# Token-major z1 and spatial product, with the gated product turned by DMA, in a fused state-space and gMLP kernel

## The chip, the cores and the metric

The kernel runs on one core of one Trainium2 chip. The metric is device microseconds (us) of that core. Before the change the median was 384.5 us over four runs (381.9 to 388.1). The run whose trace was kept took 377.6 us (a span of 375.8), less than any of these four, so comparisons with the trace of the kernel before are off by up to some 2%. Runs of one kernel scatter by 1 to 2% here; a run more than 1.5% above the fastest of its kernel is called slow, and ratios use fast runs alone: the mean time of one kernel's fast runs over the mean of the other's in the same rounds, so a ratio is not quite the quotient of the medians quoted beside it.

Engines: PE is the tensor engine (PEld its weight loads), DVE the vector engine, ACT the scalar engine, POOL is GpSimd, SP the engine whose queue issues most transfers.

## The reference, cut to what matters

```python
x = A_u                                           # [1, 2048, 640], bf16
g = sigmoid((x * gate_w).sum(-1, keepdims=True))
a = ssm_conv(x, ...)                              # long convolution, done by FFT
z = gelu(x @ w_in)                                # [2048, 1728]
z1 = z[..., :864];  z2 = layernorm(z[..., 864:])
s = einsum('ts,bsf->btf', w_sp, z2) + b_sp[None, :, None]     # the spatial product, [2048, 864]
b = (z1 * s) @ w_out                              # [2048, 640]
return g * a + (1 - g) * b
```

`a` needs tables of complex exponentials (DVE, ACT and POOL make them in four parts), a transform of the tables, and a convolution. `b` is nearly all matmuls. The kernel weaves the two together: the matmuls of `b` fill PE while the tables are made.

## The kernel before

Every piece of work is a task with an assumed cost. A planner in the kernel file plays the tasks through once, when the kernel is built, and fixes the order of instructions on each engine. At run time each engine follows its list in order, waiting where data or a buffer is missing. The parts that the change touches:

```python
class Plan:
    SYNC = 0.12                      # assumed wait between engines
# ...
def z1_tile(ft, hf):                 # features on partitions: 7 tiles of 128 (the last of 96), 2 halves of tokens
    # ...
    pe.matmul(ps()[0:fs, h, :], lhsT=Win1[:, i, 128*ft:128*ft+fs], rhs=xT[:, i, 1024*hf+512*h:...+512], ...)
    # GELU into zt, stored to z1_d in 512-byte rows
# ...
def sp_block(tb):                    # 8 blocks of 256 tokens
    # wT: the transposed rows of w_sp; z1t: z1 from z1_d; br: the biases as a row
    for st in range(c0, c0 + 4):
        pe.matmul(ps()[0:fs, ft - f0, :], lhsT=z2n[:, st, 128*ft:128*ft+fs], rhs=wT()[:, st, :], ...)
    if c0 + 4 == NS:                 # the bias: a product one row deep
        pe.matmul(ps()[0:fs, ft - f0, :], lhsT=ones[0:1, 0:fs], rhs=br()[:], start=False, stop=True)
    # ...
    vec.tensor_tensor(out=v_()[:], in0=ps()[:], in1=z1t()[:, f0:f0 + 2, :], op=ALU.mult)
    # v_ has features on partitions: it is the stationary operand of the output product as it stands
    pe.matmul(ps()[:], lhsT=vT[ft // 2]()[0:fs, ft % 2, 128*r:128*r+128], rhs=Wout[0:fs, ft, ...], ...)
```

## Time and profile before

| | before |
|---|---|
| span of the profiled run | 375.8 us |
| PE, DVE, ACT, POOL busy | 327.5, 281.4, 249.9, 163.5 us |
| mean granted PE clock | 0.971 |
| spatial product | 896 matmuls of 256 columns and 56 bias matmuls |
| four batches of table transforms (`ps_k`) start at | 128.2, 164.8, 213.2, 255.9 us |
| 480-wide convolution products `p` on DVE, first to last start | 265.1 to 328.3 us |

### The profile page before, as it was taken

To read this page: it belongs to the slowest core of one execution; us is meant where nothing else is said; L and a number is where in the kernel's file an instruction comes from. 1 tells how busy PE (TensorE), PEld (TensorE's weight loads), DVE (VectorE), ACT (ScalarE), POOL (GpSimd) and SP (SyncE) were. 2 spreads that over 40 slices of the span, in tenths; PEclk is the share of its full clock that TensorE was granted. 3 is DMA by queue.
4 is the path that set the end of the run, shared out by engine and by line. 5 is a ranking of instruction groups with operands and counts; after the bars stand their busy time and mean duration, and the time that the engine had idled before them with its cause. 6 is when DMAs were issued, how large, how long until landed. Compare 5 with 4: busy or idle time off the path is not lost.

```text
span 375.8 us, 9357 instructions
## 1 busy us (share of the span) xinstructions
PE 327.5 (87%) x3688; PEld 229.6 (61%) x3688; DVE 281.4 (75%) x554; ACT 249.9 (67%) x474; POOL 163.5 (44%) x167
## 2 busy tenths in 40 slices
PE   0897799995999989997899979997998999999981
PEld 0353344442777867776777857676675775788750
DVE  3298999874699999996489956892546676877574
ACT  3443955667998889995797968631246666767573
POOL 5265889990639884624512155300659200000000
PEclk9999999999899999998999989999699999999997
DMA  8794157899967035383679843694474856211364
GB/s 211 152 173 174 44 166 225 262 280 246 197 181 182 4 70 128 80 187 69 148 128 319 162 103 79 105 258 151 75 180 128 240 165 228 65 37 54 106 179 104
DMA packets 96325, 56.83 MB, mean 151 GB/s; under 512 B 66580, under 2 KB 91856, under 8 KB 96280
## 3 DMA queue, kind: packets, MB, share of 16 engines
q1 hardware_dynamic: 92264, 47.84, 51.7%
q0 software_dynamic: 4016, 8.39, 8.6%
q8 instruction: 29, 0.48, 0.6%
q14 instruction: 16, 0.13, 0.1%
HBM read 24.73 MB, written 19.47 MB: 118 GB/s over the span
## 4 chain that ended last, share of the span: by engine, by line
PE 45%; DVE 21%; DMA 10%; ACT 7%; issue 6%; SPq 5%; POOL 5%; DVEq 0%; POOLq 0%; ACTq 0%
PE ps_g L643 10%; PE ps_z L578 7%; PE ps_o L665 6%; SPq L306 5%; PE ps_v L973 4%; PE ps_s2k L961 3%; PE ps_z L549 3%; PE ps_k L799 2%; DMA fu<-FU_d 2%; PE ps_k L800 2%; DVE ET L782 2%; DMA bs<-in_B_b_sp_dram 2%; DMA obr<-ob_d 2%; ACT ET L311 2%; PE ps_s1k L885 2%
## 5 line engine op out<-in xcount | busy, mean ns | idle before, releaser
L643 PE MATMUL ps_g<-wT,z2n 128*128 128x256 bf16 (+1 forms) x896 | 118.1, 279 | 7.9 <-DVE ma L721 5.1
L643 PEld LDWEIGHTS <-z2n 128*128 128x128 bf16 (+1 forms) x896 | 88.7, 104 | 27.5 <-issue 8.7
L963 DVE TENSOR_TENSOR p<-ps_s2k,us 128x960 bf16<-128x960 f32 (+1 forms) x48 | 48.5, 1042 | 22.7 <-PE ps_s2k L961 10.9
L318 ACT CAST us<-ps_u 128x480 bf16<-128x480 f32 (+1 forms) x44 | 22.6, 526 | 31.0 <-PE ps_u L950 20.6
L977 ACT CAST vt<-ps_v 120x512 bf16<-120x512 f32 (+1 forms) x48 | 27.6, 586 | 15.9 <-PE ps_v L973 15.7
L549 PE MATMUL ps_z<-Win,xT 128*128 128x432 bf16 (+1 forms) x160 | 32.9, 363 | 3.7 <-DVE gl L558 2.4
L665 PE MATMUL ps_o<-Wout,vT 128*128 128x320 bf16 (+1 forms) x224 | 35.1, 304 | 0.0
L578 PE MATMUL ps_z<-xT,Win 128*128 128x512 bf16 (+1 forms) x140 | 33.8, 379 | 0.0
L311 ACT ACTIVATE mr<-lre 128x160 bf16<-128x160 f32 x128 | 31.6, 323 | 0.0
L973 PE MATMUL ps_v<-G,p 128*120 128x128 bf16 (+1 forms) x384 | 29.2, 220 | 0.8 <-DVE p L963 0.3
L973 PEld LDWEIGHTS <-p 128*120 128x120 bf16 (+1 forms) x384 | 26.7, 127 | 4.6 <-DVE p L963 1.4
L549 PEld LDWEIGHTS <-xT 128*128 128x128 bf16 x160 | 16.1, 101 | 20.5 <-issue 8.5
L306 POOL DMA_DIRECT2D FK_d<-s1k x14 | 13.5, 967 | 34.4 <-ACT s1k L318 18.5
L665 PEld LDWEIGHTS <-vT 128*128 128x128 bf16 (+1 forms) x224 | 21.8, 99 | 8.7
L255 POOL TENSOR_SCALAR si<-th 128x160 int32<-128x160 f32 x25 | 16.8, 673 | 23.1 <-ACT mr L311 19.2
L311 ACT ACTIVATE ET<-ci 128x640 bf16<-128x640 int16 x36 | 25.0, 727 | 1.8 <-DVE ci L255 1.8
L311 ACT ACTIVATE z2n<-ps_z 128x864 bf16<-128x864 f32 x16 | 14.2, 891 | 17.5 <-PE ps_z L549 13.3
L799 PE MATMUL ps_k<-ET 128*32 128x33 bf16 x640 | 20.7, 238 | 5.2 <-issue 5.1
L257 POOL TENSOR_SCALAR z2n<-z2n,mv,rstd 128x864 bf16<-128x864 bf16 x7 | 24.8, 3553 | 0.3
L961 PE MATMUL ps_s2k<-fk,T 128*128 128x480 bf16 (+1 forms) x128 | 24.4, 307 | 0.3 <-ACT ot L1177 0.3
L578 PEld LDWEIGHTS <-Win 128*128 128x128 bf16 (+1 forms) x140 | 14.2, 101 | 15.7 <-issue 1.1
L800 PEld LDWEIGHTS <-ET 128*32 128x32 bf16 x640 | 19.7, 143 | 5.8 <-issue 5.8
(176 smaller groups left out, 677.3 us busy)
## 6 DMA issues: line engine op xcount, KB each, us to landing
FK_d<-s1k POOLq DMA_DIRECT2D x14, 320.0 KB, 5.2
FU_d<-s1u SPq DMA_DIRECT2D x16, 240.0 KB, 3.8
fu<-FU_d SPq DMA_DIRECT2D x16, 240.0 KB, 4.1
fk<-FK_d SPq DMA_DIRECT2D x16, 240.0 KB, 4.1
z_d<-zt SPq DMA_DIRECT2D x6, 512.0 KB, 4.9
z1t<-z_d SPq DMA_DIRECT2D x8, 384.0 KB
xf<-in_A_u_dram SPq DMA_DIRECT2D x8, 320.0 KB, 3.9
ob_d<-ob SPq DMA_DIRECT2D x12, 160.0 KB, 3.8
```

The lines of the kernel that those rows point to most:

```text
L306: E_[e].dma_start(out=out_(), in_=in_())
L311: return add("ACT", cost, lambda e: act.activation(out=out_(), in_=in_(), func=func, scale=scale), r=r, w=w, fset=fs, bias=bias, deps=deps)
L549: pe.matmul(ps()[:, h, 0:432 + h], lhsT=xT[:, i, 128 * st:128 * st + 128], rhs=Win2[:, i, 432 * h:432 * h + 432 + h], start=(i == 0), stop ...
L578: pe.matmul(ps()[0:fs, h, :], lhsT=Win1[:, i, 128 * ft:128 * ft + fs], rhs=xT[:, i, 1024 * hf + 512 * h:1024 * hf + 512 * h + 512], start= ...
L643: pe.matmul(ps()[0:fs, ft - f0, :], lhsT=z2n[:, st, 128 * ft:128 * ft + fs], rhs=wT()[:, st, :], start=(st == 0), stop=False)
L665: pe.matmul(ps()[:], lhsT=vT[ft // 2]()[0:fs, ft % 2, 128 * r:128 * r + 128], rhs=Wout[0:fs, ft, HD * h:HD * h + HD], start=(ft == 0), sto ...
L799: pe.matmul(o_, lhsT=X["ET"][:, 0:32, d], rhs=X["M2"][:, :, d], start=True, stop=False, tile_position=(0, 32 * q))
L800: pe.matmul(o_, lhsT=X["ET"][:, NA:NA + 32, d], rhs=X["E2"][:, :, d], start=False, stop=True, tile_position=(0, 32 * q))
L961: pe.matmul(ps()[:, i, W * n:W * n + W], lhsT=TK(k + n, i), rhs=fk()[:, j + n, :], start=True, stop=True)
L963: add("DVE", dv1(2 * NW), lambda e, p12=p12, ps=ps, ua=ua: vec.tensor_tensor(out=p12()[:, :, 0:NW], in0=ps()[:, :, 0:NW], in1=ua().unsquee ...
L973: pe.matmul(pv()[0:CH, 128 * (NK * c + n):128 * (NK * c + n) + 128], lhsT=p12()[:, i, W * n + CH * c:W * n + CH * c + CH], rhs=GV(k + n, i ...
L977: (vec.tensor_copy if e == "DVE" else act.copy)(out=X["vt"][h][0:CH, :, :, 4 * k:4 * k + 4 * NK], in_=pv()[0:CH, :].rearrange("p (c z m) - ...
```

## The change

The intent is to cut PE's work. z1 and the spatial product are made with tokens on partitions: 432 columns per matmul instead of 256, no partly filled seventh feature tile, and the bias, now one number per partition, is added in the DVE operation that multiplies by z1. The price is that the gated product v now has tokens on partitions and must be turned before the output product: a transposing DMA from SBUF to SBUF, one per 128 tokens. v has one buffer. The core of the diff:

```diff
-    def z1_tile(ft, hf):
+    def z1_tile(st):
-                    pe.matmul(ps()[0:fs, h, :], lhsT=Win1[...], rhs=xT[...512 columns], ...)
+                    pe.matmul(ps()[:, h, 0:432], lhsT=xT[:, i, 128 * st:128 * st + 128], rhs=Win1[:, i, 432 * h:432 * h + 432], ...)
+        zt = sbt(lambda: eev, "zt", "zt", [P, Fh], bufs=3)
...
+    def sp_tile(n):
+        wT = sbt(lambda: gsp, "wT", "wT", [P, NS, P], bufs=4)
+        dma("SP", lambda: z1t()[:], lambda: z1v[:, n, :], ..., r=[("z1", st) for st in range(NS)], ...)
+        v_ = sbt(lambda: gsp, "v", "v", [P, 896], bufs=1)
+        add("POOL", 0.2, lambda e: pool.memset(v_()[:, Fh:896], 0.0), w=[(v_, "p")], bias=9000)
+                        pe.matmul(ps()[:, 0:432], lhsT=wT()[:, st, :], rhs=z2n[:, st, 432 * h:432 * h + 432], ...)
+            vec.scalar_tensor_tensor(out=v_()[:, 432 * h:...], in0=ps()[:, 0:432], scalar=bsf[:, n:n + 1],
+                in1=z1t()[:, 432 * h:...], op0=ALU.add, op1=ALU.mult)
+        vT = sbt(lambda: gsp, "vT", "vT", [P, 7, P], bufs=2)
+            dma("SP", lambda: vT()[:], lambda: v_()[:], 229000, r=vr, w=[vT], tr=True, bias=5000)
...
-            pv = (gps if k % 99 == 0 else xps)("ps_v", [P, 512])
+            pv = (gps if k % 1 == 0 else xps)("ps_v", [P, 512])
```

(Cut: names, costs, unchanged arguments and the numbers of buffers. Also cut: the planner's priority of the DVE operation that makes v, and of the operation that takes the output product out of PSUM, falls from 9500 to about 400. The last pair moves the convolution's `ps_v` to the PSUM banks that the spatial product uses.)

More of the change, by code (lines that the diff above doesn't have):

```diff
@@ L279 @@
     KB_d = [dram.tile([129, w], BF, name=f"KB_d{g}") for g, w in enumerate(KW)]
-    z1_d = dram.tile([8, P, NFT, 256], BF, name="z1_d")
+    z1_d = dram.tile([L, Fh], BF, name="z1_d")
+    v_d = dram.tile([NS, P, 896], BF, name="v_d")
     ob_d = dram.tile([P, NS, D], BF, name="ob_d")
-    br_d = dram.tile([NS, P], BF, name="br_d")
     ctx.enter_context(tc.manual_schedule())
@@ L337 @@
     short = sbpool(short_s, "short", 1, "right")
-    for nm, n in (("dummy", 1), ("kk", 2), ("ti", 2), ("two", 2), ("g", 2), ("x", 2), ("wT", 2), ("z1t", 2), ("vT", 4), ("ob", 2), ("br", 2),
-                  ("xf", 2), ("s1u", 5), ("zt", 2), ("bst", 2), ("jk", 2), ("kg", 1)):
+    for nm, n in (("dummy", 1), ("kk", 2), ("ti", 2), ("two", 2), ("g", 2), ("x", 2), ("wT", 4), ("z1t", 3), ("vT", 2), ("v", 1), ("ob", 2),
+                  ("xf", 2), ("s1u", 5), ("zt", 3), ("bst", 2), ("jk", 2), ("kg", 1)):
         ring(nm, n)
@@ L410 @@
     c64 = bits("c64", 6, 1)
-    ones = const.tile([1, P], BF, name="ones")
-    vec.memset(ones[:], 1.0)
     mhalf = const.tile([P, NS], F32, name="mhalf")
@@ L448 @@
     vec.memset(gl[:, NS:32], 0.0)
-    bt16 = early.tile([NS, P], BF, name="bt16")
+    bsf = const.tile([P, NS], F32, name="bsf")
     psm = xps("pt_s", [P, 1024], BF)
     add("PE", 0.1, lambda e: pe.transpose(out=psm()[:, 0:ND], in_=gw5[:], identity=ident[0:ND, 0:ND]), r=["gw5", "pre3"], w=[psm], bias=6000)
-    add("PE", 0.1, lambda e: pe.transpose(out=psm()[0:NS, 128:256], in_=bs16[:], identity=ident[:]), r=["bs16"], w=[(psm, 1)], bias=6000)
     S_(add("DVE", 0.2, lambda e: vec.tensor_copy(out=Win2[:, :, Fh:Fh + 1], in_=psm()[:, 0:ND].unsqueeze(2)), r=[psm], w=["gwt"], bias=6000))
-    add("DVE", 0.2, lambda e: vec.tensor_copy(out=bt16[:], in_=psm()[0:NS, 128:256]), r=[(psm, 1)], w=["bt16"], bias=6000)
-    dma("POOL", lambda: br_d[:], lambda: bt16[:], 4096, r=["bt16"], w=["br_d"])
+    E(add("POOL", 0.3, lambda e: pool.tensor_copy(out=bsf[:], in_=bs16[:]), r=["bs16"], w=["bsf"], bias=3000))
     th = parm.tile([P, D], F32, name="th")
@@ L568 @@
     z1_ids, z2_ids, xb = [], {}, {}
-    XB = {13: 38}
-    def z1_tile(ft, hf):
-        fs = fsz[ft]
+    XB = {15: 38}
+    def z1_tile(st):
         ps = two("ps_z1")
@@ L577, in m @@
                 for i in range(ND):
-                    pe.matmul(ps()[0:fs, h, :], lhsT=Win1[:, i, 128 * ft:128 * ft + fs], rhs=xT[:, i, 1024 * hf + 512 * h:1024 * hf + 512 * h + 512],
+                    pe.matmul(ps()[:, h, 0:432], lhsT=xT[:, i, 128 * st:128 * st + 128], rhs=Win1[:, i, 432 * h:432 * h + 432],
                               start=(i == 0), stop=(i == ND - 1))
-            E(add("PE", 5 * mm(512), m, r=["Win1", ("xT", 2 * hf + h)], w=[(ps, h)], bias=3000 - 100 * (2 * ft + hf) - h))
-        if hf == 0:
-            zth[ft] = sbt(lambda: eev, "zt", "zt", [P, NS, P], bufs=2)
-        zt = zth[ft]
-        z1_ids.append(actf(ac(1024), lambda: zt()[0:fs, :, 64 * hf:64 * hf + 64].rearrange("f n (e p) -> f n e p", e=2),
-                           lambda: ps()[0:fs, :, :].rearrange("f e (p n) -> f n e p", n=NS), ACT.Gelu_apprx_tanh, [(ps, 0), (ps, 1), "dt16", "pre"], [(zt, hf)], bias=9000, deps=next((xb[t] for t in range(2 * ft + hf, -1, -1) if t in xb), [])))
-        if hf == 1:
-            E(dma("SP", lambda: z1_d[:, 0:fs, ft, :].rearrange("b p t -> p b t"), lambda: zt()[0:fs, :, :].rearrange("f (b r) t -> f b (r t)", r=2), 524000, r=[(zt, 0), (zt, 1)],
-                   w=[("z1", tb, ft) for tb in range(8)], bias=5000, run=512))
-    zth = {}
+            E(add("PE", 5 * mm(432), m, r=["Win1", ("xT", st // 4)], w=[(ps, h)], bias=3000 - 100 * st - h))
+        zt = sbt(lambda: eev, "zt", "zt", [P, Fh], bufs=3)
+        z1_ids.append(actf(ac(864), lambda: zt()[:].rearrange("p (e f) -> p e f", e=2), lambda: ps()[:, :, 0:432], ACT.Gelu_apprx_tanh,
+                           [(ps, 0), (ps, 1), "dt16", "pre"], [zt], bias=9000, deps=next((xb[t] for t in range(st, -1, -1) if t in xb), [])))
+        E(dma("SP", lambda: z1_d[128 * st:128 * st + 128, :], lambda: zt()[:], 221000, r=[zt], w=[("z1", st)], bias=5000, run=1728))
     xfh = {}
@@ L621 @@
     wspv = B_w_sp.rearrange("(p n) s -> p n s", n=NS)
-    brv = br_d[:].rearrange("n p -> (n p)").unsqueeze(0)
+    z1v = z1_d[:].rearrange("(p n) f -> p n f", n=NS)
     def sp_block(tb):
-        wT = sbt(lambda: gsp, "wT", "wT", [P, NS, 256])
-        for r in range(2):
-            dma("SP", lambda r=r: wT()[:, :, 128 * r:128 * r + 128], lambda r=r: wspv[:, 2 * tb + r, :], 540000, r=["xf3"], w=[(wT, r)], tr=True, bias=1000 - 100 * tb)
-        z1t = sbt(lambda: gsp, "z1t", "z1t", [P, NFT, 256])
-        dma("SP", lambda: z1t()[:, 0:6, :], lambda: z1_d[tb, :, 0:6, :], 393000, r=[("z1", tb, f) for f in range(6)], w=[(z1t, 0)], bias=1000 - 100 * tb, run=3072)
-        dma("SP", lambda: z1t()[0:96, 6, :], lambda: z1_d[tb, 0:96, 6, :], 49000, r=[("z1", tb, 6)], w=[(z1t, 1)], bias=1000 - 100 * tb, run=512)
-        br = sbt(lambda: gsp, "br", "br", [1, 256])
-        dma("SP", lambda: br()[:], lambda: brv[:, 256 * tb:256 * tb + 256], 512, r=["br_d"], w=[br], bias=1000 - 100 * tb)
-        vT = []
-        for f0 in range(0, NFT, 2):
-            ps = gps("ps_g", [P, 2, 256])
-            fts = range(f0, min(NFT, f0 + 2))
-            for ft in fts:
-                fs = fsz[ft]
-                for c0 in range(0, NS, 4):
-                    def m(e, ft=ft, fs=fs, ps=ps, f0=f0, c0=c0):
-                        for st in range(c0, c0 + 4):
-                            pe.matmul(ps()[0:fs, ft - f0, :], lhsT=z2n[:, st, 128 * ft:128 * ft + fs], rhs=wT()[:, st, :], start=(st == 0), stop=False)
-                        if c0 + 4 == NS:
-                            pe.matmul(ps()[0:fs, ft - f0, :], lhsT=ones[0:1, 0:fs], rhs=br()[:], start=False, stop=True)
-                    add("PE", (4 + (c0 + 4 == NS)) * mm(256), m, r=([(wT, 0), (wT, 1), br] if c0 == 0 else [wT, br]) + ([(ps, f0)] if ft > f0 and c0 == 0 else []) + [("z2n", s) for s in range(c0, c0 + 4)], w=[(ps, ft)], bias=-1000 - 100 * tb)
-            v_ = sbt(lambda: gsp, "vT", "vT", [P, 2, 256], bufs=4)
-            if f0 < 6:
-                add("DVE", dv1(512), lambda e, v_=v_, ps=ps, f0=f0: vec.tensor_tensor(out=v_()[:], in0=ps()[:], in1=z1t()[:, f0:f0 + 2, :], op=ALU.mult),
-                    r=[(ps, f) for f in fts] + [(z1t, 0)], w=[v_], bias=9500)
-            else:
-                add("DVE", dv1(256), lambda e, v_=v_, ps=ps: vec.tensor_tensor(out=v_()[0:96, 0, :], in0=ps()[0:96, 0, :], in1=z1t()[0:96, 6, :], op=ALU.mult),
-                    r=[(ps, f) for f in fts] + [(z1t, 1)], w=[v_], bias=9500)
-            vT.append(v_)
-        for r in range(2):
-            n = 2 * tb + r
-            late = tb >= 6
-            ob = (lambda n=n: X["obx"][:, n - 12, :]) if late else sbt(lambda: gsp, "ob", "ob", [P, D])
-            for h in range(2):
-                ps = xps("ps_o", [P, HD])
-                def m(e, r=r, h=h, ps=ps):
-                    for ft in range(NFT):
-                        fs = fsz[ft]
-                        pe.matmul(ps()[:], lhsT=vT[ft // 2]()[0:fs, ft % 2, 128 * r:128 * r + 128], rhs=Wout[0:fs, ft, HD * h:HD * h + HD],
-                                  start=(ft == 0), stop=(ft == NFT - 1))
-                add("PE", 7 * mm(HD), m, r=vT + ["Wout0", "Wout1"] + (["vap"] if late else []), w=[ps], hold_=[] if late else [ob], bias=-1000 + 5 - 100 * tb)
-                add("ACT", 0.53, lambda e, ob=ob, h=h, ps=ps, n=n: act.activation(out=ob()[:, HD * h:HD * h + HD], in_=ps()[:], func=ACT.Copy, scale=omg[:, n:n + 1]),
-                    r=[ps, "omg"], w=[("obx", n, h) if late else (ob, h)], bias=9500)
-            if not late:
-                dma("SP", lambda ob=ob, n=n: ob_d[:, n, :], lambda ob=ob: ob()[:], 164000, run=1280, r=[(ob, 0), (ob, 1)], w=[("ob", n)])
@@ new lines, in sp_block, with m @@
+        for n in (2 * tb, 2 * tb + 1):
+            sp_tile(n)
+    def sp_tile(n):
+        B0 = -50 * n
+        wT = sbt(lambda: gsp, "wT", "wT", [P, NS, P], bufs=4)
+        dma("SP", lambda: wT()[:], lambda: wspv[:, n, :], 540000, r=["xf3"], w=[wT], tr=True, bias=1000 + B0)
+        z1t = sbt(lambda: gsp, "z1t", "z1t", [P, Fh], bufs=3)
+        dma("SP", lambda: z1t()[:], lambda: z1v[:, n, :], 221000, r=[("z1", st) for st in range(NS)], w=[z1t], bias=1000 + B0, run=1728)
+        v_ = sbt(lambda: gsp, "v", "v", [P, 896], bufs=1)
+        add("POOL", 0.2, lambda e: pool.memset(v_()[:, Fh:896], 0.0), w=[(v_, "p")], bias=9000)
+        for h in range(2):
+            ps = gps("ps_g", [P, 512])
+            for c0 in range(0, NS, 4):
+                def m(e, ps=ps, c0=c0, h=h):
+                    for st in range(c0, c0 + 4):
+                        pe.matmul(ps()[:, 0:432], lhsT=wT()[:, st, :], rhs=z2n[:, st, 432 * h:432 * h + 432], start=(st == 0), stop=(st == NS - 1))
+                add("PE", 4 * mm(432), m, r=[wT] + [("z2n", s) for s in range(c0, c0 + 4)], w=[ps], bias=-1000 + B0)
+            add("DVE", dv1(432), lambda e, ps=ps, h=h: vec.scalar_tensor_tensor(out=v_()[:, 432 * h:432 * h + 432], in0=ps()[:, 0:432], scalar=bsf[:, n:n + 1],
+                in1=z1t()[:, 432 * h:432 * h + 432], op0=ALU.add, op1=ALU.mult), r=[ps, z1t, "bsf"], w=[(v_, h)], bias=400 + B0)
+        vT = sbt(lambda: gsp, "vT", "vT", [P, 7, P], bufs=2)
+        vr = [(v_, "p"), (v_, 0), (v_, 1)]
+        if False:
+            dma("SP", lambda: v_d[n], lambda: v_()[:], 229000, r=vr, w=[("vd", n)], bias=5000, run=1792)
+            dma("SP", lambda: vT()[:], lambda: v_d[n], 229000, r=[("vd", n)], w=[vT], tr=True, bias=5000)
+        else:
+            dma("SP", lambda: vT()[:], lambda: v_()[:], 229000, r=vr, w=[vT], tr=True, bias=5000)
+        late = n >= 12
+        ob = (lambda: X["obx"][:, n - 12, :]) if late else sbt(lambda: gsp, "ob", "ob", [P, D])
+        for h in range(2):
+            ps = xps("ps_o", [P, HD])
+            def m(e, h=h, ps=ps):
+                for ft in range(NFT):
+                    fs = fsz[ft]
+                    pe.matmul(ps()[:], lhsT=vT()[0:fs, ft, :], rhs=Wout[0:fs, ft, HD * h:HD * h + HD], start=(ft == 0), stop=(ft == NFT - 1))
+            add("PE", 7 * mm(HD), m, r=[vT, "Wout0", "Wout1"] + (["vap"] if late else []), w=[ps], hold_=[] if late else [ob], bias=-1000 + 50 + B0)
+            add("ACT", 0.53, lambda e, h=h, ps=ps: act.activation(out=ob()[:, HD * h:HD * h + HD], in_=ps()[:], func=ACT.Copy, scale=omg[:, n:n + 1]),
+                r=[ps, "omg"], w=[("obx", n, h) if late else (ob, h)], bias=400 + B0)
+        if not late:
+            dma("SP", lambda: ob_d[:, n, :], lambda: ob()[:], 164000, run=1280, r=[(ob, 0), (ob, 1)], w=[("ob", n)])
@@ L993 @@
     done_ = []
-    for i in range(2 * NFT):
-        z1_tile(i // 2, i % 2)
+    for i in range(NS):
+        z1_tile(i)
         if i < 8:
@@ L1053 @@
     kg2_s = ExitStack()
-    add("NONE", 0.0, open_cvt, w=["cvt"], deps=early_ids, r=["HT", "br_d", "gwt", "bt16"])
+    add("NONE", 0.0, open_cvt, w=["cvt"], deps=early_ids, r=["HT", "bsf", "gwt"])
     t_ids = []
```

## The prediction

> **What bounds the kernel now.** I read the page first (busy shares, slices, groups), then the stretches of 20 us, the tensor engine's waits and timeline, then the transposes. The page says that the tensor engine (PE) is the fullest, and that the spatial product is its largest user:
>
> ```profile
> PE 327.5 (87%) x3688; PEld 229.6 (61%) x3688; DVE 281.4 (75%) x554; ACT 249.9 (67%) x474; POOL 163.5 (44%) x167
> ...
> PE   0897799995999989997899979997998999999981
> ...
> DVE  3298999874699999996489956892546676877574
> ...
> L643 PE MATMUL ps_g<-wT,z2n 128*128 128x256 bf16 (+1 forms) x896 | 118.1, 279 | 7.9 <-DVE ma L721 5.1
> ```
>
> The reader is to see a PE row of nines from slice 10 on, and one group, L643 (the spatial product), with a third of PE's busy time. It is spread as filler from 94.7 us to 328.1 us, beside the tables (DVE nearly full from 120 to 160 us) and then beside the convolution. In the view by stretches:
>
> ```profile
> 140.00:160.00 20.00, 19.56 (x158) 14.99 (x156) 19.79 (x40) 18.81 (x30) 9.94 (x7) 1.00 0.46 109
> ...
> 280.00:300.00 20.00, 18.74 (x172) 13.37 (x171) 13.17 (x13) 12.49 (x24) 13.88 (x25) 1.00 0.68 188
> 300.00:320.00 20.00, 19.05 (x174) 13.32 (x173) 13.43 (x13) 12.50 (x24) 0.89 (x1) 1.00 0.63 201
> ```
>
> The columns are start:end and length, then busy us of PE, PEld, DVE, ACT, POOL, then clock, DMA share and GB/s. PE has 19 of 20 us in the convolution stage, where DVE and ACT have 13: there PE sets the pace, and each us of filler taken away shortens the stage. Before 90 us the chain of waits runs through z1 on PE; after about 345 us the end is evictions and output, which the change does not touch.
>
> The busy sum overstates PE, since ends of pipelined matmuls are modelled. So I take start-to-start distances from PE's timeline:
>
> ```profile
> 199.08 1.91 PE L643 MATMUL ps_g<-wT,z2n 128*128 128x256 bf16 x16
> 200.92 0.28 PE L645 MATMUL ps_g<-br,ones 1*128 1x256 bf16 x1
> 201.13 0.61 PE L643 MATMUL ps_g<-wT,z2n 128*128 128x256 bf16 x4
> 201.67 0.28 PE L645 MATMUL ps_g<-br,ones 1*128 1x256 bf16 x1
> 201.88 0.72 PE L885 MATMUL ps_s1k<-xk,F 128*128 128x320 bf16 x4
> ```
>
> Here the columns are start us, us to the last end, engine, line and group. Sixteen products take 1.84 us until the bias matmul (L645, one row deep) starts, and four take 0.54 us. The difference, 1.30 us for twelve, is 108 ns each; the fixed rest is about 0.1 us, and the bias matmul then holds PE for 0.21 us more. So one bias matmul costs about 0.3 us, three times a real product of the same width. That is the largest thing that the change removes.
>
> **What the Trainium skill says.** "TensorE: Matmul & The Clock Gate", section Back-to-back issue gap, gives N/2.4 + 2.5 ns for a warm isolated gap: 109.2 ns for 256 columns, 182.5 for 432, 215.8 for 512. The trace agrees: 108 ns above, and in the chain ten z1 matmuls of 512 columns take 2.16 us. That section has nothing on the bias matmul; 0.3 us is the trace's. "DMA: Bandwidth & Descriptors", section DMA Transpose (X-bar), asks for a destination in SBUF, 2-byte type and partitions in multiples of 16; the new transpose (128 rows of 896 bf16) fits. The same page, section Latency and other measured facts, gives 261 GB/s for a transposing DMA; this trace is slower, 524288 bytes per 2.79 us of the queue's time, 188 GB/s, so I use the trace:
>
> ```profile
> L304 SPq DMA_TRANSPOSE wT<-in_B_w_sp_dram x16: 2087/2791/4768, 82.5 to 244.1; - x16
> ...
> DMA to landing us min/median/max: 4.7/5.7/6.0
> ```
>
> **The change part by part.** All 16 token tiles now have their own spatial product of 2 x 16 matmuls of 432 columns, and the result has tokens on partitions.
>
> Spatial product on PE. Before: 896 x 109 ns = 97.7 us, plus 56 bias matmuls x 0.3 us = 16.8 us, together 114.5. After: 512 x 182.5 ns = 93.4 us; the bias goes into the DVE operation. Saved: 21.1 us. About 3.5 us of it is the padding of the seventh tile (96 of 128 rows used), about 17 the bias.
>
> z1 on PE. Before: 140 x 216 = 30.2 us. After: 160 x 182.5 = 29.2 us. Saved: 1.0 us, in the stage from 52 to 90 us where PE is on the chain. Weight loads are not a new limit: 97 ns each for xT, hidden below 182 ns. ACT: 14 x 1.024 = 14.3 us becomes 16 x about 0.89 (z2's duration for the same 864 elements) = 14.2 us.
>
> Output product: 224 matmuls of 320 columns, unchanged.
>
> DVE. Before: 24 x 0.691 + 8 x 0.410 = 19.9 us. After: 32 scalar_tensor_tensor of 432 from PSUM. The kernel's own one of 480 (L1151) takes 0.713 us, so about 0.66 us each, 21 us. Added: 1.2 us.
>
> DMA. z1 goes out and in with rows of 1728 bytes instead of 512 out: slightly better in the stretch from 82 to 95 us, where the DMA share is 1.01. New are 16 transposes of 128 x 896, 224 KB. The two transposes in the trace, 160 KB (1.27 us of queue, 3.5 us to landing) and 512 KB (2.79 and 5.7), give by a straight line about 1.55 us of queue and 3.9 us to landing. The SP queue has room: 16 x 1.55 = 25 us against over 190 us that it spends waiting. None is on a DMA limit, but each stands between a product and its output product, which used to need one DVE operation of 0.7 us.
>
> Smaller parts. The bias transpose and its trip through DRAM disappear from the start, where PE runs the gate's transpose at 11.0 us and the bias's at 11.3: about 0.3 us. The first product waits 5.1 us before 94.7 us; the second half of wT was issued at 89.15 us and lands 5.7 us later, at 94.8, so that is the true releaser. One token tile of wT now suffices. But all of z1 must have been stored before the first z1t can load, so the two ps_g buffers fill (5.8 us) and PE waits for DVE instead: I count nothing. ps_v moves to the other pair of PSUM banks, away from ps_u and ps_o: a small gain, also not counted.
>
> PE work removed: 21.1 + 1.0 + 0.3 = 22.4 us.
>
> How much arrives at the end? Between 95 and 340 us PE is busy some 94% of the time, but in the table stage it shares the lead with DVE and ACT. The filler saved there moves filler forward out of the convolution stage, which has about 24 us of ps_g work and 6 us of ps_o. Without it that stage comes near its own floor: 32 x 1.153 us of DVE for p and about as much ACT (0.562 + 0.589 per step), some 37 us, against about 63 us now. So the stage can give most of 22 us, but not with full overlap; I choose 75%, 17 us.
>
> Against it: sixteen waits for a turned tile. v has a single buffer, so tile n+1 is multiplied only after the transpose of tile n has landed: 3.9 us plus 1.3 us of DVE, 5.2 us, against 5.8 us of products per tile. That fits, with 0.6 us to spare. The order of instructions is fixed when the kernel is built, so a late transpose stalls PE. Also, the SP queue is in order: a transpose that waits for DVE, or issues for 1.55 us, delays the fu and fk loads, which are issued just as buffers come free. I take 0.3 us a tile, an estimate without a row to support it: 5 us. Net: 17 - 5 = 12 us, 386.1 - 12 = 374 us.
>
> **The rivals.**
>
> *The turn becomes the bound.* If a transpose from SBUF lands in 7 us instead of 3.9, the single v buffer makes each tile 8.3 us and PE stands for 1 to 2 us per tile, 16 to 30 us: time 380 to 395. For it: every transpose in this trace reads DRAM, none SBUF. Against it: sixteen tiles over some 235 us leave 14.7 us each, and SP is mostly waiting.
>
> *DVE and ACT keep the table stage and the convolution chain as long as now.* Then the PE time becomes idle time and the kernel stays at 382 to 388. For it: DVE has 19.8 to 20 of 20 us from 120 to 160 us. Against it: in the convolution stage they have 13 of 20 while PE has 19.
>
> *The saving arrives whole*, because the start gap also closes and ps_v no longer shares buffers: 386 - 22 - 3 = 361. For it: 5.1 us of idle PE at 90 us. Against it: z1t's dependence on all of z1.
>
> **Range and chances.** The middle is 374. The runs before scatter from 381.9 to 388.1, and the profiled run took 377.6, so 2 us either way is noise. The range goes from nearly the whole saving to nearly none: 363 to 386. Faster by over 2% means below 378.4: I give 0.66. Within 2%: 0.24, if waits eat most of it. Slower: 0.10, the first rival at its worst.
>
> **What would show it.** PE's matmuls: the line of the spatial product with x512, start-to-start near 182 ns, no L645; its busy time about 100 us, PE's in all lower by some 20 us. The z1 stage shorter by 1 us. The new transposes near 1.5 us on SP and 4 us to landing. The convolution stage shorter than 63 us. The prediction is wrong if PE shows long waits for the turned tile or for v, if the landing is above 6 us, or if PE's busy time falls by 20 us and the span does not.

## More of the kernel before

The transforms are short matmuls that can only run when a part of the tables is complete, so their dates show how fast the tables come. From the page of the kernel before, ACT by slices of a fortieth of the span, the granted clock and the DMA share:

```profile
ACT  3443955667998889995797968631246666767573
PEclk9999999999899999998999989999699999999997
DMA  8794157899967035383679843694474856211364
```

A digit is tenths of the slice; 9 in the clock row is full speed. The clock row has only single dips.

## The result, and the profile after

The changed kernel took 399.4 us (median of four runs, 395.9 to 400.9) against 384.5: a ratio of 1.0398, interval 1.0286 to 1.0509. It is slower by 4%, where 374 us (363 to 386) was predicted. From the page after, the busy shares, the slices and the spatial product:

```profile
span 394.1 us, 8573 instructions
...
PE 318.9 (81%) x3267; PEld 192.6 (49%) x3267; DVE 280.5 (71%) x553; ACT 251.2 (64%) x478; POOL 162.0 (41%) x195
...
PE   0897799996799889988784969865587998999982
...
DVE  3498999863489979996765764568744457888764
...
PEclk9999999999699999998897878889669899999987
...
L631 PE MATMUL ps_g<-z2n,wT 128*128 128x432 bf16 x512 | 109.3, 368 | 14.7 <-DVE v L633 14.5
```

The reader is to see that the work itself did not grow: PE has 421 matmuls fewer, DVE and ACT are busy as long as before. PE's row has new holes (a 4, and later 65587) where it had mostly nines, and the clock row has many 8s, 7s and 6s. The mean granted clock fell from 0.971 to 0.925. The same stretches as the prediction showed, and the emptiest one, after:

```profile
140.00:160.00 20.00, 19.02 (x143) 11.08 (x143) 16.44 (x41) 17.59 (x39) 10.28 (x12) 1.00 0.50 113
...
260.00:280.00 20.00, 9.76 (x43) 4.52 (x42) 16.02 (x24) 5.78 (x9) 2.30 (x4) 0.84 0.58 163
280.00:300.00 20.00, 16.85 (x399) 12.07 (x397) 9.78 (x13) 6.91 (x14) 6.25 (x10) 0.74 0.47 103
300.00:320.00 20.00, 17.51 (x129) 10.85 (x127) 8.48 (x10) 11.28 (x22) 15.82 (x30) 0.91 0.60 161
```

From 260 to 280 us PE is busy for 9.76 of 20 us. By its view of waits the stops there are 3.3 us for DVE's making of v, 4.1 us for a load (`fk`) and 3.0 us for DVE's making of v again. The columns are as in the prediction.

The timeline of PE after shows that the cost of a product was foreseen rightly: sixteen products take 2.92 us from start to the next group's start, 182.5 ns each.

```profile
213.99 4.48 PE L631 MATMUL ps_g<-z2n,wT 128*128 128x432 bf16 x12 [4.49 <-DVE v L633]
218.26 0.97 PE L869 MATMUL ps_s1k<-xk,F 128*128 128x320 bf16 x4
219.07 3.08 PE L631 MATMUL ps_g<-z2n,wT 128*128 128x432 bf16 x16
221.99 0.71 PE L869 MATMUL ps_s1k<-xk,F 128*128 128x320 bf16 x4
```

But the first line shows a stop of 4.49 us, and twelve products after it take 4.27 us instead of 2.19. By windows of 4 us the clock there is:

```profile
208.00:212.00 4.00, 0.87 (x6) 0.49 (x6) 1.30 (x2) 2.55 (x5) 1.00 (x2) 1.00 1.00 244
212.00:216.00 4.00, 2.02 (x6) 0.84 (x6) 2.74 (x5) 0.66 (x1) 0.88 (x2) 0.50 1.12 277
216.00:220.00 4.00, 4.00 (x17) 1.88 (x16) 4.00 (x3) 1.04 (x3) 0.00 (x0) 0.65 0.82 209
```

The clock is 1.00, then 0.50, then 0.65. The Trainium skill, "TensorE: Matmul & The Clock Gate", section Part 1: The HAM clock gate, says that PE's clock is halved after an idle window of about 3.4 us and released after as long a busy one. The trace agrees here: the clock goes to 0.50 in a stop of 4.49 us, which ends at 213.99, and 0.65 in the last window is the mean of a part at half and a part at full clock. So this stop of PE is paid a second time, by 2.1 us in these twelve products.

What held PE and DVE at that moment is in two timelines after the change, the SP queue's first, then DVE's:

```profile
197.91 8.39 SPq L306 DMA_DIRECT2D xk<-KA_d  x8
...
208.18 1.43 SPq L304 DMA_TRANSPOSE vT<-v  x1
```

```profile
195.00 1.24 DVE L633 SCALAR_TENSOR_TENSOR v<-ps_g,bsf,z1t 128x432 bf16<-128x432 f32 x2 [0.54 <-DMA vT<-v]
...
213.26 1.24 DVE L633 SCALAR_TENSOR_TENSOR v<-ps_g,bsf,z1t 128x432 bf16<-128x432 f32 x2 [3.96 <-DMA vT<-v]
```

v was complete at 196.2 us. Its transpose stood in the SP queue behind the loads of the tables (`xk`), at one of which the queue itself stood for 3.6 us, and was issued at 208.2 us, 12 us later; it landed at about 213.2. Until then the only buffer of v was taken, DVE stood 3.96 us in front of the next product, and with it the table work behind that product in DVE's list. PE's two PSUM banks for the product stayed full, so PE stood as well. The transpose by itself is as quick as foreseen, from the view of that tile:

```profile
L304 SPq DMA_TRANSPOSE vT<-v x16: 1221/1240/1495, 101.7 to 327.2; - x16
...
DMA to landing us min/median/max: 2.9/3.7/5.9
```

(durations of the queue in ns: least, median, most). From the views of waits of DVE, of POOL and of PE, with the total, the number and the longest in us:

```profile
DVE v L633 <- DMA vT<-v: 8.2, 3, 4.0
```

```profile
POOL v L625 <- DMA vT<-v: 19.3, 7, 4.5
```

```profile
PE ps_g L631 <- DVE v L633: 14.5, 4, 6.4
```

POOL writes the zero pad of each v and so stands for the same buffer. The dates of the table transforms, with two later runs of the same layout that have no such wait of DVE (they are explained below):

| batch of `ps_k` starts at (us) | 1 | 2 | 3 | 4 | from 4 to the end |
|---|---|---|---|---|---|
| before | 128.2 | 164.8 | 213.2 | 255.9 | 119.9 |
| changed | 133.5 | 174.0 | 227.3 | 280.7 | 113.4 |
| later by | 5.3 | 9.2 | 14.1 | 24.8 | -6.5 |
| two v and five z1 buffers | 132.3 | 172.6 | 221.0 | 270.1 | 112.6 |
| turn on PE (five rounds) | 135.5 | 173.1 | 227.6 | 270.7 | 109.2 |

The starts of the fourth batch in these four runs, in this order:

```profile
255.89 0.27 PE L799 MATMUL ps_k<-ET 128*32 128x33 bf16 x4
280.70 0.27 PE L783 MATMUL ps_k<-ET 128*32 128x33 bf16 x4
270.08 0.27 PE L783 MATMUL ps_k<-ET 128*32 128x33 bf16 x4
270.74 0.27 PE L789 MATMUL ps_k<-ET 128*32 128x33 bf16 x4 [8.64 <-DVE ET L762]
```

The delay grows over the whole table stage. After it the changed kernel gains a little back (its filler is done at 335 us instead of 352), and 18.3 us of span remain. But a late date is not yet a loss: the turn on PE has dates nearly as late, and by its times it is 1% faster than before. Only the part by which the changed kernel is later than the run with two v and five z1 buffers, 1.3, 1.4, 6.3 and 10.6 us, goes with the buffers; the rest came with the new layout and its order of instructions, and half of it or more is made up after the fourth batch.

### The profile page after: what moved, and what is told of

Same layout as the page of the kernel before. It is cut to its first block, busy times and chain, and to the rows that moved or that the text cites.

```text
span 394.1 us, 8573 instructions
## 1 busy us (share of the span) xinstructions
PE 318.9 (81%) x3267; PEld 192.6 (49%) x3267; DVE 280.5 (71%) x553; ACT 251.2 (64%) x478; POOL 162.0 (41%) x195
## 4 chain that ended last, share of the span: by engine, by line
PE 41%; DVE 19%; DMA 13%; issue 8%; ACT 8%; POOL 6%; SPq 3%; DVEq 0%; POOLq 0%; ACTq 0%
PE ps_g L631 13%; PE ps_z L573 4%; PE ps_o L650 4%; PE ps_v L957 4%; DVE p L947 3%; PE ps_k L783 3%; PE ps_z L545 3%; DMA vT<-v 3%; PE ps_k L784 3%; PE ps_s2k L945 2%; DMA xk<-KA_d 2%; SPq L306 2%; DMA xk<-KB_d 2%; DMA gw<-in_gate_w_dram 2%; DVE ET L766 2%
## 5 line engine op out<-in xcount | busy, mean ns | idle before, releaser
L631 PE MATMUL ps_g<-z2n,wT 128*128 128x432 bf16 x512 | 109.3, 368 | 14.7 <-DVE v L633 14.5
L631 PEld LDWEIGHTS <-wT 128*128 128x128 bf16 x512 | 52.3, 103 | 61.8 <-issue 25.8
L650 PE MATMUL ps_o<-Wout,vT 128*128 128x320 bf16 (+1 forms) x224 | 36.5, 314 | 2.7 <-DMA vT<-v 2.2
L633 DVE SCALAR_TENSOR_TENSOR v<-ps_g,bsf,z1t 128x432 bf16<-128x432 f32 x32 | 20.7, 662 | 23.8 <-PE ps_g L631 14.2
L318 ACT CAST us<-ps_u 128x480 bf16<-128x480 f32 (+1 forms) x41 | 20.8, 536 | 25.8 <-PE ps_u L934 18.4
L957 PE MATMUL ps_v<-G,p 128*120 128x128 bf16 (+1 forms) x384 | 30.5, 225 | 5.0 <-DVE p L947 2.8
L573 PE MATMUL ps_z<-Win,xT 128*128 128x432 bf16 x160 | 32.8, 346 | 0.0
L945 PE MATMUL ps_s2k<-fk,T 128*128 128x480 bf16 (+1 forms) x128 | 26.0, 318 | 4.2 <-DMA fk<-FK_d 4.1
L784 PE MATMUL ps_k<-ET 128*32 128x33 bf16 x640 | 21.2, 236 | 5.1 <-issue 5.1
L783 PE MATMUL ps_k<-ET 128*32 128x33 bf16 x640 | 21.0, 238 | 5.1 <-issue 4.8
L318 ACT CAST s1k<-ps_s1k 128x640 bf16<-128x640 f32 x20 | 13.5, 693 | 18.1 <-PE ps_s1k L869 12.7
L311 ACT ACTIVATE z2n<-ps_z 128x864 bf16<-128x864 f32 x16 | 14.1, 890 | 16.7 <-PE ps_z L545 13.8
```

The costliest lines, as they stand in the source:

```text
L311: return add("ACT", cost, lambda e: act.activation(out=out_(), in_=in_(), func=func, scale=scale), r=r, w=w, fset=fs, bias=bias, deps=deps)
L318: (vec.tensor_copy if e == "DVE" else act.copy)(out=out_(), in_=in_())
L573: pe.matmul(ps()[:, h, 0:432], lhsT=xT[:, i, 128 * st:128 * st + 128], rhs=Win1[:, i, 432 * h:432 * h + 432], start=(i == 0), stop=(i == N ...
L631: pe.matmul(ps()[:, 0:432], lhsT=wT()[:, st, :], rhs=z2n[:, st, 432 * h:432 * h + 432], start=(st == 0), stop=(st == NS - 1))
L650: pe.matmul(ps()[:], lhsT=vT()[0:fs, ft, :], rhs=Wout[0:fs, ft, HD * h:HD * h + HD], start=(ft == 0), stop=(ft == NFT - 1))
L783: pe.matmul(o_, lhsT=X["ET"][:, 0:32, d], rhs=X["M2"][:, :, d], start=True, stop=False, tile_position=(0, 32 * q))
```

## The experiments

Two theories stood at first. A: the turned tile is the cost, through v's single buffer and the transpose's place in an in-order queue. B: the turn is harmless, and the cost comes from the other parts, the coarser product, the wait for all of z1, or the banks of `ps_v`. For the missing gain there was C: PE was never the limit, so removing its filler buys nothing. Later D was added: the planner's order is a matter of luck, and before is a lucky one. One rival was not tested: the priority of making v, which the change lowered (see the diff), may have moved the tables as well.

"Same order" means that the planner saw the old numbers, so every engine has the same instructions in the same order, and only the buffer really allocated differs.

**A second buffer for v, same order.**

```diff
-        v_ = sbt(lambda: gsp, "v", "v", [P, 896], bufs=1)
+        v_ = sbt(lambda: gsp, "v", "v", [P, 896], bufs=2)      # planner still told 1
```

> The changed kernel with a second buffer for v, in the same planned order of instructions, so only the wait of the next tile's product (and of its pad) for the transpose of the tile before is taken away. Theory A (the single buffer, with transposes that are issued 7 to 12 us late in the in-order SP queue, stops DVE, GpSimd and then PE): 8 to 15 us faster than the changed kernel (about 385 to 391), mean clock above 0.94. Rival B (the waits of DVE for products and the slow clock stand by themselves): within 3 us of 399.

Median 390.3 us, ratio 1.0147 (1.0001 to 1.0294), against 1.0398 for the changed kernel: 2.5% less, about 10 us. That is what A asked for, at its low side. The clock of its three fast runs was 0.935 to 0.957, on average above the 0.94 expected.

**The same, and the planner may reorder** (`("v", 1)` becomes `("v", 2)`).

> The same second buffer, and the planner knows of it and may reorder. Theory A: as fast as the run with the same order or up to 5 us faster (380 to 390). Rival B: within 3 us of 399.

Median 403.3 us, ratio 1.0512 (1.0396 to 1.0628). A miss for A as stated: DVE's wait for v is gone in this order too (POOL still stands 29.8 us for it), but PE now waits for the loads of the tables, which it hardly did before (1.8 us in 3 waits):

```profile
PE ps_s1k L869 <- DMA xk<-KA_d: 14.8, 4, 7.2
```

The longest of these loads took 10.4 us to land here, against 4.2 before the change and 8.4 in the changed kernel.

**The kernel before without its bias matmuls** (wrong result), same order.

```diff
-                            ... start=(st == 0), stop=False)
-                        if c0 + 4 == NS:
-                            pe.matmul(ps()[0:fs, ft - f0, :], lhsT=ones[0:1, 0:fs], rhs=br()[:], start=False, stop=True)
+                            ... start=(st == 0), stop=(st == NS - 1))
```

> The kernel before without its 56 bias matmuls (wrong result on purpose), same order. My prediction's sum (0.3 us each, 16.8 us, of which 75% arrive): 11 to 14 us faster than before. Rival C (table stage set by DVE and ACT, PE's filler is slack there): 0 to 5 us faster although PE's busy sum falls by more than 10 us.

Median 382.6 us beside 387.0, ratio 0.9895 (0.9707 to 1.0083): some 4 us, not clear of noise. The interval reaches from 3 us slower to 11 us faster, so by the times alone only the upper part of the expected 11 to 14 us is excluded. PE's busy time fell by 12.2 us, from 327.5:

```profile
PE 315.3 (83%) x3632; PEld 229.3 (61%) x3632; DVE 280.6 (74%) x554; ACT 249.4 (66%) x474; POOL 161.3 (43%) x167
```

The trace shows where the freed time went. In the views of PE's waits, this is what PE stood for the multiplication by z1, before and here:

```profile
PE ps_g L643 <- DVE vT L649: 1.8, 5, 0.8
```

```profile
PE ps_g L643 <- DVE vT L647: 7.5, 10, 1.5
```

All of PE's waits for DVE together grew from 13.5 to 21.2 us. The transforms start at 128.4, 164.2, 213.0 and 258.2 us, as before within 2.3 us, and the 480-wide products run from 266.8 to 331.3 us, 64.5 us instead of 63.2. Against the kept trace of before no stage became shorter; since that trace is of a run 6 us faster than the mean of the fast runs of before beside this one (383.6 us), a saving of 4 us could hide there, but hardly one of 12. This speaks for C: most of the twelve us of PE work turned into waiting.

**`ps_v` back in its old banks** (`k % 1` becomes `k % 99`, replanned).

> The changed kernel with ps_v back in the banks of ps_u and ps_o. If ps_v's sharing of banks with ps_g costs time: 4 us or more faster than 399. If the move helped as the plan meant: 2 us or more slower. Theories A and B: within 3 us of 399.

Median 396.3 us, ratio 1.035 (1.0188 to 1.0511). No difference that the runs can tell (and the order changed with it), so the loss of 4% is not due to this part.

**No turn at all**, same order: the output product reads v as it stands (wrong result), v has four buffers.

```diff
-            dma("SP", lambda: vT()[:], lambda: v_()[:], 229000, r=vr, w=[vT], tr=True, bias=5000)
+            add(("SP",), [0.3], lambda e: X.__setitem__(("v", n), v_()), ...)      # a task that issues nothing
-                    pe.matmul(ps()[:], lhsT=vT()[0:fs, ft, :], rhs=Wout[...], ...)
+                    pe.matmul(ps()[:], lhsT=X[("v", n)][0:fs, 128 * ft:128 * ft + 128], rhs=Wout[...], ...)
```

> The changed kernel with the transpose taken out: the output product reads v as it stands (wrong result on purpose), v has four buffers, all other instructions keep their order. Theory A (the turn by DMA, its latency and its place in the in-order SP queue, is the cost): 10 to 18 us faster than the changed kernel, 381 to 389, i.e. at or below the kernel before. Rival B (the cost lies in the coarser product and in the waits for z1, which are still there): 0 to 6 us faster than 399, still above before. The ratio to before of the run with two v buffers was 1.015: what is below that is what the output product's and the other queues' waits for the turned tile add.

Median 383.1 us beside 387.7, ratio 1.0032 (0.988 to 1.0183). Taking the turn away removes the loss, 3.7% of 4.0%, about 14 us. But that leaves the kernel level with before (from 4.6 us faster to 7 us slower), although it has the layout's cheaper PE work without the turn. This agrees with C, but less strictly than the run before: the order of instructions is not that of the kernel before.

**Five buffers for the z1 tile**, same order (`bufs=3` becomes `bufs=5` in `zt`).

> The changed kernel with five buffers for the z1 tile instead of three, same order. The trace of the changed kernel shows the last GELU waiting 4.3 us for a store of z1, which starts the tables 2.5 us later. If that delay is carried to the end: 2 to 4 us faster than the changed kernel, first exponential table before 91.5 us. If another wait takes its place (z1 loads): under 1 us.

Median 399.5 us, ratio 1.0496 (1.0358 to 1.0635). The wait it was made for is gone (the last GELU starts at 89.6 us instead of 92.1, and the first exponential tables at 91.8 instead of 94.3), and nothing of it arrives; the waits for v are longer instead, 38.7 us beside 27.6 in the changed kernel. From the view of v, what its readers and writers stood for in this run, in us and times:

```profile
  DMA vT<-v: 38.7, 11
```

**Two v buffers and five z1 buffers**, same order.

> The changed kernel with two v buffers and five z1 buffers, same order. If the two waits add up: ratio to before 1.00 to 1.01 (384 to 389). If only the v wait counts: 1.015, as the run with two v buffers.

Median 385.6 us, ratio 1.0094 (0.9937 to 1.0251), in the range expected if the two waits add up, though the interval holds 1.015 too. This run and the one before it ran on one chip and differ in one number, v's buffers: 399.5 against 385.6, 14 us. In the same view of v, no wait for the transpose is left, only the ordinary one for the product (and 2.1 us for a load of z1):

```profile
  PE ps_g L631: 16.6, 8
```

In this order of instructions the single buffer is thus shown to be the cost. The late issue alone is not: in this run, by the timelines of DVE and SP, five of the sixteen transposes are issued 7 to 19 us after their v is complete, as late as in the changed kernel, and with a second buffer DVE and POOL no longer stand for it.

**The turn on PE**: seven PE transposes and one copy from PSUM instead of the DMA, two v buffers, replanned.

```diff
-            dma("SP", lambda: vT()[:], lambda: v_()[:], 229000, r=vr, w=[vT], tr=True, bias=5000)
+            pt = xps("pt_w", [P, 1024], BF)
+            # PE: seven pe.transpose of 128 columns of v_ into pt
+            evac(("ACT", "DVE"), 896, lambda: vT()[:]..., lambda: pt()[:, 0:896], [pt], [vT], ...)
```

> The changed kernel with the tile turned by seven PE transposes and one copy from PSUM instead of by DMA, two v buffers, replanned. Theory A: the wait goes, 14 us of ACT or DVE work and about 8 us of PE work come: 380 to 392. Rival B: 395 or more. It could beat the kernel before only if the added evictions stay in gaps of ACT.

Median 378.7 us beside 387.7, ratio 0.9876 (0.9683 to 1.007), just below the range expected by A. Run again in five rounds:

> The turn on PE once more, in five rounds, for a verdict: 0.98 to 0.995 of before, 376 to 382 us; faster by over 2% only if the first run's 0.9876 was low by chance the other way.

Median 379.7 us beside 384.6, ratio 0.9899 (0.9843 to 0.9955): 1% below before, clear of noise but small. The view of the turned tile in this run:

```profile
L645 PE MATMUL pt_w<-ident,v x112: 217/219/314, 102.3 to 299.4; 128*128 128x128 bf16 x112
L318 DVE COPY vT<-pt_w x11: 610/624/626, 103.3 to 300.7; 128x896 bf16<-128x896 bf16 x11
L318 ACT COPY vT<-pt_w x5: 906/906/907, 130.7 to 299.3; 128x896 bf16<-128x896 bf16 x5
```

The turn costs DVE 11 x 0.624 = 6.9 us and ACT 5 x 0.906 = 4.5 us of work, and no trip through the queue. POOL still stands 26.6 us for v here, longer than in the changed kernel, so POOL's wait by itself is no sign of loss. This run also shows the tables holding PE: in the view by stretches, just before the fourth batch, DVE is busy with the tables all the time and PE stands still.

```profile
262.00:270.70 8.70, 0.09 (x1) 0.00 (x0) 8.70 (x9) 1.53 (x3) 0.89 (x1) 0.66 0.41 123
```

**The turn on PE with five z1 buffers**, in that order and replanned.

> The turn on PE with five z1 buffers instead of three, same order as the turn on PE. If the two gains add as they did beside two v buffers (1.0147 to 1.0094): ratio to before 0.975 to 0.985, about 376. If the tables wait for something else there: as the turn on PE, 0.9876.

> The turn on PE with five z1 buffers known to the planner, which then reorders. It should be within 2% of the run in the old order (372 to 388); the spread between the two says how much the order alone is worth.

The first: median 380.1 us, ratio 0.977 (0.9693 to 0.9847), but that ratio rests on two of six runs, which go from 373.4 to 385.3, and its median is no better than 379.7 with three buffers, so no gain of the buffers is claimed. The second: 388.8 us, ratio 1.012 (1.0056 to 1.0185). The order alone moved the kernel by 3.5%, which is as much as the whole question.

**The turn planned ahead of the table loads**: the transposing DMA's priority goes from 5000 to 20000, one v buffer, replanned.

> The changed kernel, one v buffer, but the transposing DMA planned ahead of the table loads (xk, KA, KB) in the SP queue; the planner reorders. If the late issue in the queue (7 to 12 us at three tiles) is most of the wait: 4 to 10 us faster than the changed kernel (389 to 395). If the single buffer with 3.7 us of landing is enough to make the wait, or the displaced xk loads cost as much: within 3 us of 399 or slower.

Median 397.4 us, ratio 1.0358 (1.0298 to 1.0417). All transposes but one are now issued within 2.3 us of a complete v, DVE's wait for the transpose nearly vanished (0.8 us in one wait; POOL's is 10.4), and the time did not move: PE's wait for `xk` is 10.4 us here and for `fk` 7.6. So an early issue does not cure the loss by itself, in this new order. Who stands first in the queue changes who waits.

These last results asked for D. The planner's assumed wait between engines (`SYNC`, 0.12 us) was set to 0.11 and 0.13, which changes nothing but the order drawn.

> The kernel before in another order (the planner's assumed wait between engines 0.11 us instead of 0.12). If the change itself costs 4% (theory A): within 2% of before. If order is most of it (rival D: before is a lucky order): 2 to 5% slower than before, like the changed kernel.

> The same with 0.13 us. A: within 2% of before. D: 2 to 5% slower.

> The changed kernel in another order, 0.11 us. A: 3 to 5% slower than before, as the changed kernel. D: anywhere between 0 and 6% slower, overlapping the redrawn orders of before.

> The same with 0.13 us. A: 3 to 5% slower than before. D: anywhere between 0 and 6%, overlapping the redrawn orders of before.

> Two v buffers, known to the planner, in the order of 0.11 us. If the single buffer is the cost in any order: 385 to 395. If the turn by DMA costs through the queue also with two buffers: 398 to 410, as the first replanned run (403).

> The turn on PE in the order of 0.11 us. If the DMA turn is the cost: 376 to 392, below every order of the changed kernel. If the good runs on PE were order luck: 395 or more.

| design | medians of its orders, us | ratios of fast runs to before |
|---|---|---|
| before | 384.5, 385.3, 397.8 | 1, 1.014, 1.031 |
| changed (one v) | 399.4, 410.5, 400.5 | 1.040, 1.070, 1.058 |
| two v, replanned | 403.3, 400.4 | 1.051, 1.049 |
| turn on PE (third with five z1 buffers) | 379.7, 393.6, 388.8 | 0.990, 1.028, 1.012 |

(For the first four of the six runs the ratios are worked out here from the fast runs: the before beside them had two, 378.3 and 380.3 us; the 1.031 rests on one fast run of 391.0, and its other three took 397.6 to 399.6.) D is half true: an order is worth 3 to 4% to the same design, and before is the best of its three. Several expectations missed: the changed kernel at 7.0% lies above both A's and D's, at 5.8% above A's, before at 3.1% is what D asked for, and the turn on PE at 393.6 us is just above its 392. The mean ratio is 1.015 for before, (1.040 + 1.070 + 1.058) / 3 = 1.056 for the changed kernel, and 1.010 for the turn on PE. So the change costs about 4% on average over orders, but with three orders of each, which scatter by 1.5%, this is uncertain by some 3.5% (an estimate from the spread of these ratios). The ratios of the two designs do not overlap, though the medians of the slowest before (397.8 us) and the fastest changed kernel (399.4) nearly meet. Turning on PE instead takes the loss back on average. A second buffer takes it back in the old order only.

## Why the prediction was wrong

The price list was right. A product of 432 columns takes 182.5 ns, as stated. The DVE operation takes 0.662 us, stated 0.66. The transpose takes 1.24 us of queue and 3.7 us to landing, stated 1.55 and 3.9. The bias matmuls are gone, and without them alone PE's busy time fell by 12.2 us, of 16.8 stated (the statement was of time from start to start). The z1 stage did not become 1 us shorter: from the first z1 matmul to the `pt_f` transposes it takes 37.5 us in both. PE's busy time fell by 8.6 us instead of some 20; the spatial product shows 109.3 us instead of about 100 because part of it ran at a lowered clock (its products show 346 ns at the median and up to 567).

The first step that failed is "there PE sets the pace, and each us of filler taken away shortens the stage", with the choice of 75%, 17 us. Removing the bias matmuls alone left the stages about as long as they were and made PE wait instead, and the version without any turn, which has the whole PE saving, is level with before. Measured in place of 17: about 4 us for the bias matmuls (from -3 to 11), and about zero for the layout without its turn (from 4.6 us faster to 7 us slower, in another order). Much of the busy PE in the stretches was filler in the gaps of a chain through the tables on DVE and ACT, the transforms, the loads and the convolution. That chain is read from the traces: no run made DVE or ACT faster. Nor was PE never the limit, as C was first put: on the page of before, in the chain of work that ended last, PE has 45% of the span and the spatial product 10%. That was the second rival, "DVE and ACT keep the table stage and the convolution chain as long as now", 382 to 388 us; without the turn the runs gave 383. The argument used against it, 13 of 20 us busy in the convolution stage, was the wrong test: an engine at two thirds can be on the chain at every step.

The second is the step "I take 0.3 us a tile ... 5 us". The term was mis-sized: by the run without the turn it is about 14 us, 0.9 us a tile. The reasoning "that fits, with 0.6 us to spare" set 5.2 us against 5.8 us and started the clock when v was complete. At five tiles the transpose was issued 7 to 17 us after that (6.8, 11.9, 13.3, 9.7 and 17.2 by the timelines of DVE and SP; the expectations say three), behind other loads in the queue. With one buffer, every such delay holds the next tile. And a wait of one tile is not paid by PE alone: DVE stands in front of the buffer with the table work behind it, and PE restarted at half the clock after the stop shown above. The first rival named this wait ("makes each tile 8.3 us"; by its own numbers PE would then stand 2.5 us a tile, not 1 to 2) but looked for its cause in a longer landing; the landing was short, the standing in the queue was long.

How the slow clock shares in the loss stays open: it is lower where PE stops more (0.925 in the changed kernel, 0.952 with two v and five z1 buffers, 0.971 before), but the turn on PE is faster than before at 0.952, and no run held the clock and kept the stops. It also stays open through which wait the DMA turn costs its 4% in the redrawn orders. There the traces show waits for loads: PE waits for `xk`, `fk`, `fu` and `vT` total 4.8 us before and in its third order, 11.9 in the changed kernel, 27.6 in its second order and 28.4 with two v replanned, against 2.7 with the turn on PE (17.8 in the latter's second order). But this sum does not rank the runs: it is 18.4 us with two v and five z1 buffers, which is 1% above before, and the third order of before is 3% slower with the same 4.8. That the transposes hold up those loads, and that this is the 4%, is a guess that no run settles.

No version beats before by a margin that an order of instructions could not also give. The best, the turn on PE in its first order, is 1% faster.

## What to carry to other kernels

A full engine is the limit only if work removed from it shortens the stage: before counting on it, remove a piece of the work as a test, even with a wrong result, and see whether the time falls or the engine waits. Dates (when does each stage's first dependent instruction start?) tell where a delay arises, but not whether it reaches the end. A transfer put between two engines is late by what its queue makes of it, not by its latency alone; here a second buffer bore that lateness, and a single one passed it on to the engines whose lists touch the buffer. Where the order of instructions is drawn by a planner, compare a few orders of both kernels before believing a difference of 3 or 4%.

## What the Trainium skill lacked or had wrong

- "DMA: Bandwidth & Descriptors", section Latency and other measured facts, gives 261 GB/s for a transposing DMA and 350 to 400 when contiguous. Here 224 KB from SBUF to SBUF took 1.24 us of the queue, 229376 bytes / 1.24 us = 185 GB/s, and 512 KB from DRAM 188 GB/s by the same measure, which is the time that the queue was held and not that of the transfer alone; landing took 3.7 us (median) for 224 KB.
- The same page, section Rules for kernel authors, tells to issue early and wait late, but not that a transfer is issued late when it stands behind others in its issuing engine's list: here 12 us from v's completion to the issue of its transpose.
- "TensorE: Matmul & The Clock Gate", section Part 4: PE-mode transpose, gives about 275 ns for a 128 x 128 bf16 transpose in a kernel; the profile here shows 219 ns (median of 112).
- The same page, section Back-to-back issue gap, fits the products (182.5 ns for 432 columns) but has nothing on a matmul one row deep among full ones, which held PE for about 0.3 us in the kernel before.
- No page that was read says how much the order of instructions alone can move a kernel: here 3.1% for before and 3.8% for the turn on PE (0.990 and 1.028).
